# Probabilities with adjoining key columns for each transpose, and mask matmuls of 64 columns

## The chip, the cores and the metric

The kernel runs on one core of a Trainium2 chip. The time is the device time of one execution in microseconds (us), the median of several runs. The engines run beside each other: TensorE (PE; its weight loads are shown as PEld), VectorE (DVE), ScalarE (ACT), GpSimd (POOL) and SyncE (SP), whose queue issues the transfers.

## What is computed

Three layers follow each other: an attention whose scores get a bias from a running sum, a gated feed-forward layer that also mixes along the sequence, and a second layer that mixes along the sequence with a cosine and a sine part. The change is in the attention alone (B, H, S, D = 4, 8, 576, 64):

```python
scores = scale * np.matmul(q, k.transpose(0, 1, 3, 2))
causal = np.triu(np.ones((S, S), dtype=bool), k=1)
cum = np.cumsum(np.maximum(s, 0.0), axis=-1)
bias = -(cum[:, :, :, None] - cum[:, :, None, :])
scores = np.where(causal, -1e9, scores + np.minimum(bias, 0.0))
attn = np.exp(scores - np.max(scores, axis=-1, keepdims=True))
attn = attn / (np.sum(attn, axis=-1, keepdims=True) + 1e-09)
x = np.matmul(attn, v)
```

Then x goes through the feed-forward layer (x @ w_in, Gelu, a normed gate mixed by w_sg, @ w_out, plus x), and through theta = x @ w_theta, the sequence mixing of x cos(theta) and x sin(theta), and a last product with w_ch.

## The kernel before

Float32 products are made of float32r parts, a rounded high part and the rest: three matmuls for each product (high by low, low by high, high by high). All of them are recorded at one line (L106), so they are told apart by their tiles.

**Attention by pairs.** The 32 heads go in 16 pairs of two; the 64 dimensions of the first head lie in partitions 0 to 63, those of the second in 64 to 127, so the score matmuls of the two heads use different rows of TensorE and run side by side. The 576 queries are cut into five row tiles t (QS, QE: first row and causal end; t = 0 has 64 rows of its own, the others 128), and a row tile has only QE[t] keys: 64, 192, 320, 448 or 576.

**Scores (`score_units`).** Two groups of tiles fill the four PSUM banks of the tile `sc` in turn: (4, 1, 0), then (3, 2). For each tile there are three products and then the mask matmuls, bf16, which add a large negative number (mlow by mpick) to the keys behind each query: two masks for t = 1 to 4 (one for each block of 64 keys on the diagonal), one for t = 0, each for both heads. So far each mask covers 128 columns, of which 64 get zeros. VectorE then takes bias and scores together (L344: C plus scores, with the row minimum into negm) into E, and ScalarE takes the exponential in place, with the row sum (L350).

**The tile E.** It holds 1600 columns for each of the two heads, the heads interleaved: `E = [P, 1600, 2]`, so that one head's columns lie 8 bytes apart.

**Transposes (`transpose_units`).** E must be turned around for the product with v. TensorE does this with an identity: 128 columns of E are loaded as weights, and the identity is streamed through (L375, 25 for each pair, into PSUM tiles T of 512 columns; one more turns the reciprocals r). Blocks are named by row tile t and key block kt (kt = 0: the first 64 keys, where both heads share one transpose: the 64 keys of two heads interleaved are 128 adjoining columns; kt = 1 to 4: 128 keys of one head). ScalarE and VectorE copy T out to Ef and E0 (L383 to L404). `pv_units` then makes the product with v0 (first 64 keys, both heads in one block-diagonal tile) and vr.

**Order.** `attention` writes the steps of pair p's scores, pair p-1's transposes and pair p-2's product in a fixed order (ORDER, ORDER_V). Between the steps `pace` takes matmuls of the feed-forward layer of the batch before, as far as a credit of estimated nanoseconds allows; there is none of it for the first four pairs. Pieces of weight conversion are put in by a plan (PLAN). The build then lays out each engine's queue with a simulated timeline (`schedule_with_timeline_sim=True`); `row` keeps the score matmuls of a group together.

**After attention**, near 335 us, the last batch's feed-forward layer, the output products (wo), theta and the second layer follow (yo, th, co); none of their lines is touched.

## Time and profile before

| | |
|---|---|
| median of 3 runs | 674.57 us (673.63 to 678.18) |
| the profiled execution | 674.18 us |
| its span, first to last instruction | 672.3 us |
| mean granted TensorE clock | 0.986 |
| busy: PE, PEld, DVE, ACT, POOL | 634.8, 556.9, 427.4, 363.2, 179.0 us |
| transfers | 83.57 MB, 124 GB/s on the mean |

The span is that of the instructions; 1.9 us of the profiled execution lie around it. Busy times add up the stretches in which at least one instruction of the engine is under way; matmuls overlap, so a row of equal ones is read by the distance between them. The 40 slices of the page are 16.8 us each; attention takes the first twenty.

### The profile page before, as it was taken

Reading aid. Unit: us, or ns where it says so; the run is one execution under the profiler, and the core shown is the slowest. Engines: PE = TensorE matmul, PEld = TensorE weight load, DVE = VectorE, ACT = ScalarE, POOL = GpSimd, SP = SyncE. Lnnn points to the kernel's source line nnn. Section 1 sums busy time; section 2 is a strip of 40 time slices with the busy share of each in tenths; the row PEclk is TensorE's granted clock in tenths of the full one; section 3 lists DMA queues with packets and bytes.
Section 4 is the critical chain, followed back from the end, with each engine's and each line's share of the span. In section 5 each row is a group of like instructions: output and inputs, shape, how many; then the busy total and the mean of one; then the engine's idle time right before and its main releaser. Section 6 shows DMA issues by size and latency. Waiting matters only on the chain.

```text
span 672.3 us, 12581 instructions
## 1 busy us (share of the span) xinstructions
PE 634.8 (94%) x4676; PEld 556.9 (83%) x4676; DVE 427.4 (64%) x1048; ACT 363.2 (54%) x836; POOL 179.0 (27%) x203
## 2 busy tenths in 40 slices
PE   5889989989999999999997888999999999999997
PEld 4666667778777888778787788898999999989997
DVE  5578856765567563773259977887773477458412
ACT  3767768774688844775155435565550454245100
POOL 4234532433314423044397633220000100100000
PEclk9989999999999999999999889999999999999999
DMA  4556753266632565201355879831001200300101
GB/s 145 190 182 215 233 163 120 77 191 207 203 104 74 169 190 185 73 31 63 119 144 162 266 244 356 264 109 61 1 1 70 73 0 36 106 1 1 71 1 71
DMA packets 50189, 83.57 MB, mean 124 GB/s; under 512 B 8432, under 2 KB 20176, under 8 KB 50128
## 3 DMA queue, kind: packets, MB, share of 16 engines
q1 hardware_dynamic: 50128, 82.76, 38.4%
q8 instruction: 37, 0.61, 0.4%
q14 instruction: 24, 0.20, 0.1%
HBM read 61.61 MB, written 21.13 MB: 123 GB/s over the span
## 4 chain that ended last, share of the span: by engine, by line
PE 65%; ACT 10%; DMA 8%; DVE 8%; POOL 4%; issue 4%; SPq 1%; DVEq 0%; ACTq 0%; POOLq 0%
PE yo L106 17%; PE fo L106 13%; PE th L106 8%; PE co L106 8%; PE wo L106 6%; PE Y L106 4%; PE sc L106 4%; PE T L375 4%; ACT E L350 3%; POOL vT L653 2%; DMA wraw<-in_moe_w_tok_i 1%; PE tp L802 1%; DMA wraw<-in_moe_w_tok_r 1%; DMA wraw<-wd 1%; ACT vT L701 1%
## 5 line engine op out<-in xcount | busy, mean ns | idle before, releaser
L350 ACT ACTIVATE E<-E,negm 128x576 f32<-128x576 f32 (+4 forms) x160 | 92.8, 587 | 2.3 <-DVE negm L344 2.1
L106 PE MATMUL yo<-wkh,zh 128*128 128x288 f32 x288 | 85.3, 296 | 0.2 <-DVE x2T L875 0.2
L106 PE MATMUL yo<-wkl,zh 128*128 128x288 f32 x288 | 85.2, 296 | 0.0
L106 PE MATMUL yo<-wkh,zl 128*128 128x288 f32 x288 | 85.2, 297 | 0.0
L344 DVE CUSTOM_DVE_ANT_0 E<-sc,C 128x576 f32<-128x576 f32 (+4 forms) x160 | 68.2, 486 | 13.5 <-PE sc L106 11.3
L375 PE MATMUL T<-ident,E 128*128 128x128 f32 x400 | 64.2, 292 | 11.1 <-ACT Ef L383 5.6
L375 PEld LDWEIGHTS T<-ident,E 128*128 128x128 f32 x400 | 54.0, 193 | 17.1 <-ACT Ef L383 8.8
L106 PE MATMUL fo<-x,wih 128*128 128x288 f32 x256 | 56.0, 304 | 1.4 <-ACT uT L721 1.4
L106 PEld LDWEIGHTS yo<-wkh,zh 128*128 128x128 f32 x288 | 54.1, 188 | 0.7 <-DVE x2T L875 0.4
L106 PEld LDWEIGHTS yo<-wkl,zh 128*128 128x128 f32 x288 | 54.1, 188 | 0.3
L106 PEld LDWEIGHTS yo<-wkh,zl 128*128 128x128 f32 x288 | 54.0, 188 | 0.1
L106 PE MATMUL co<-u,wch 128*128 128x288 f32 x256 | 53.0, 295 | 0.0
L99 POOL TENSOR_SCALAR xt<-x2s 128x128 fp32r<-128x128 f32 x16 | 10.8, 688 | 155.8 <-DVE x2s L103 155.8
L106 PE MATMUL wo<-gh,woh 128*128 128x288 f32 x128 | 39.3, 310 | 8.1 <-ACT gh L95 4.7
L106 PEld LDWEIGHTS fo<-x,wih 128*128 128x128 f32 x256 | 41.8, 188 | 4.0 <-ACT uT L721 2.2
L106 PE MATMUL fo<-wih,x 128*128 128x512 f32 x128 | 43.3, 404 | 1.3 <-ACT x L95 0.7
L387 DVE COPY Ef<-T 128x512 f32<-128x512 f32 x32 | 21.8, 684 | 34.9 <-PE T L375 31.5
L106 PE MATMUL th<-wth,x2s 128*128 128x512 f32 x128 | 42.9, 400 | 0.0
L95 ACT CAST u<-x2T 128x576 fp32r<-128x576 f32 x16 | 10.7, 672 | 59.3 <-DVE x2T L875 59.3
L106 PE MATMUL sc<-kl,qh 64*128 64x288 f32 (+1 forms) x192 | 39.0, 397 | 3.0 <-DVE negm L344 3.0
L106 PEld LDWEIGHTS co<-u,wch 128*128 128x128 f32 x256 | 41.7, 188 | 0.0
L297 POOL TENSOR_TENSOR kl<-K,kh 128x576 fp32r<-128x576 f32 x15 | 21.8, 1452 | 67.2 <-ACT kh L95 36.9
(193 smaller groups left out, 1775.7 us busy)
## 6 DMA issues: line engine op xcount, KB each, us to landing
C<-cd SPq DMA_DIRECT2D x15, 576.0 KB, 6.1
Q<-in_q SPq DMA_DIRECT2D x16, 288.0 KB, 3.8
K<-in_k SPq DMA_DIRECT2D x16, 288.0 KB, 3.9
xT<-rd SPq DMA_DIRECT2D x32, 144.0 KB, 2.9
xd<-xT SPq DMA_DIRECT2D x16, 288.0 KB
gd<-uT SPq DMA_DIRECT2D x16, 288.0 KB, 4.4
gr<-gd SPq DMA_DIRECT2D x16, 288.0 KB
xr<-xd SPq DMA_DIRECT2D x16, 288.0 KB, 3.5
```

Of the source, the lines that this page charges most:

```text
L95: nc.scalar.copy(out, src)
L99: nc.gpsimd.tensor_scalar(out, src, 1.0, 1.0, op0=ALU.mult, op1=ALU.mult)
L106: return self.nc.tensor.matmul(out, lhsT, rhs, start=start, stop=stop)
L297: low = nc.gpsimd.tensor_tensor(kl, K, f32(kh), op=ALU.subtract)
L344: nc.vector.tensor_tensor_reduce(at.rearrange("p (i n) -> p i n", i=m), o[:, :, j], C[:, j, 0:n].rearrange("p (i n) -> p i n", i=m), -1.0, ...
L350: nc.scalar.activation(at, at, AF.Exp, bias=negm[:, j, c:c + 1], scale=-1.0, accum_out=sm[:, j * 5 + c:j * 5 + c + 1])
L375: nc.tensor.transpose(T[:, col:col + P], e, self.ident)
L387: nc.vector.tensor_copy(Ef[:, 512:1024], T)
L653: nc.gpsimd.tensor_scalar(vT[0:r, t], vT[0:r, t], rs[0:r, t:t + 1], nm[0:r, t:t + 1], op0=ALU.mult, op1=ALU.add)
L701: nc.scalar.activation(vT, vT, AF.Gelu_apprx_tanh)
L802: nc.tensor.transpose(tp[0:r, dt * P:(dt + 1) * P], x2T[:, dt, a:a + r], self.ident)
```

## The change

E becomes one row of 3200 columns. Of each row tile the first head's keys stand first, in blocks of 64 in falling order, then the second head's in rising order. So 128 keys of one head adjoin (the first head's two blocks swapped), and the two heads' first 64 keys meet in the middle and adjoin as well. VectorE writes the first head's blocks in falling order with a pattern of 64-column blocks. To match, the host swaps the two halves of each 128 rows of v for the even heads, and the transfers into v0 put the second head's 64 rows below the first's instead of between them. The PSUM tile `sc` gets the head as its outer index, row tile 4's two halves become adjoining columns across the border of two banks (its first half moves to column 224, row tile 1 to column 0), and each mask matmul has just the 64 columns of its own block; mpick shrinks from 192 columns to 64. Nothing is added and no order is written differently.

```diff
--- before.py
+++ after.py
@@ -28,9 +28,11 @@
 QS = [0, 64, 192, 320, 448]
 QR = [64, 128, 128, 128, 128]
 QE = [64, 192, 320, 448, 576]
-EOFF = [0, 64, 256, 576, 1024]
-
-GROUPS = [[[(4, 0, 288, 0), (1, 0, 192, 288)], [(4, 288, 288, 0), (0, 0, 64, 288)]],
+EOFF = [0, 128, 512, 1152, 2048]
+
+
+
+GROUPS = [[[(4, 0, 288, 224), (1, 0, 192, 0)], [(4, 288, 288, 0), (0, 0, 64, 288)]],
           [[(3, 0, 448, 0)], [(2, 0, 320, 0)]]]
 
 
@@ -147,7 +149,7 @@
 
 
         low = self.cum.tile([P, 2, P], F32, name="low")
-        pick = self.cum.tile([P, 3, 64], F32, name="pick")
+        pick = self.cum.tile([P, 64], F32, name="pick")
         nc.gpsimd.memset(low, 0.0)
         nc.gpsimd.memset(pick, 0.0)
         for i in (0, 64):
@@ -158,13 +160,13 @@
                     base=-64 * m, channel_multiplier=-1
                 )
             nc.gpsimd.affine_select(
-                out=pick[r, 1], in_=pick[r, 1], pattern=[[1, 64]], compare_op=ALU.not_equal, fill=NEG,
+                out=pick[r], in_=pick[r], pattern=[[1, 64]], compare_op=ALU.not_equal, fill=NEG,
                 base=0, channel_multiplier=-1
             )
         self.mlow = c.tile([P, 2, P], BF16, name="mlow")
         nc.vector.tensor_copy(self.mlow, low)
-        self.mpick = c.tile([P, 192], BF16, name="mpick")
-        nc.vector.tensor_copy(self.mpick, pick.rearrange("p m n -> p (m n)"))
+        self.mpick = c.tile([P, 64], BF16, name="mpick")
+        nc.vector.tensor_copy(self.mpick, pick)
         self.gcol = c.tile([P, 4], F32, name="gcol")
         self.halfpi = c.tile([P, 1], F32, name="halfpi")
         nc.vector.memset(self.halfpi, math.pi / 2)
@@ -282,7 +284,7 @@
         v0 = self.v0[pr % 3]
         for j in (0, 1):
             js = slice(c + j * D, c + j * D + D)
-            nc.sync.dma_start(v0.rearrange("(k i) c -> i k c", i=2)[j, :, j * D:j * D + D], self.v[b, 0:64, js])
+            nc.sync.dma_start(v0[j * D:j * D + D, j * D:j * D + D], self.v[b, 0:64, js])
         nc.sync.dma_start(vr, self.v[b, 64:576, c:c + P].rearrange("(t p) c -> p t c", p=P))
         self.vop[pr] = v0, vr
 
@@ -309,14 +311,14 @@
         C = self.cums.pop(pr)
         negm = self.negm[pr % 2]
         sm, r = self.st[pr % 2]
-        E = self.Es[pr] = self.a2.tile([P, 1600, 2], F32, name="E", tag="E")
+        E = self.Es[pr] = self.a2.tile([P, 3200], F32, name="E", tag="E")
         halves = [slice(j * D, j * D + D) for j in (0, 1)]
 
         for group in GROUPS:
             calls, sums, cost = [], [], 0.0
-            four = self.psS.tile([P, 2, 2, 512], F32, name="sc", tag="sc")
+            four = self.psS.tile([P, 2, 1024], F32, name="sc", tag="sc")
             for i, bank in enumerate(group):
-                o = four[:, i]
+                o = four[:, :, i * 512:i * 512 + 512]
                 for t, a, n, col in bank:
                     w = max(n, P)
                     qs = slice(QS[t], QS[t] + P)
@@ -329,24 +331,23 @@
                                           k == 0, k == 2 and not masks))
                     for m in masks:
                         for j, js in enumerate(halves):
-                            calls.append((o[:, j, col + w - P:col + w], self.mlow[js, m],
-                                          self.mpick[js, 64 - 64 * m:192 - 64 * m], False, m == masks[-1]))
+                            at = col + w - P + 64 * m
+                            calls.append((o[:, j, at:at + 64], self.mlow[js, m], self.mpick[js], False, m == masks[-1]))
                     if a == 0:
-                        sums.append((t, four[:, :, :, 0:n] if t == 4 else four[:, i:i + 1, :, col:col + n]))
+                        sums.append((t, four[:, :, i * 512 + col:i * 512 + col + QE[t]]))
                     cost += 3 * max(107.0, w / 2.4) + 120 * len(masks) + 120
             self.row(calls)
             for t, o in sums:
                 c = (t - 1) % 5
                 n = QE[t]
                 for j in (0, 1):
-                    at = E[:, EOFF[t]:EOFF[t] + n, j]
-                    m = o.shape[1]
+                    at = E[:, EOFF[t] + j * n:EOFF[t] + j * n + n].rearrange("p (b k) -> p b k", k=64)
                     nc.vector.tensor_tensor_reduce(
-                        at.rearrange("p (i n) -> p i n", i=m), o[:, :, j],
-                        C[:, j, 0:n].rearrange("p (i n) -> p i n", i=m), -1.0, BIG,
+                        at if j else at[:, ::-1], o[:, j].rearrange("p (b k) -> p b k", k=64),
+                        C[:, j, 0:n].rearrange("p (b k) -> p b k", k=64), -1.0, BIG,
                         ALU.add, ALU.min, negm[:, j, c:c + 1])
                 for j in (0, 1):
-                    at = E[:, EOFF[t]:EOFF[t] + n, j]
+                    at = E[:, EOFF[t] + j * n:EOFF[t] + j * n + n]
                     nc.scalar.activation(at, at, AF.Exp, bias=negm[:, j, c:c + 1], scale=-1.0,
                                          accum_out=sm[:, j * 5 + c:j * 5 + c + 1])
             if group is GROUPS[-1]:
@@ -370,9 +371,8 @@
 
         def transposed(T, j, blocks):
             for col, t, kt in blocks:
-                c = EOFF[t] + QS[kt]
-                e = E[:, c:c + P, j] if kt else E[:, c:c + 64].rearrange("p n j -> p (n j)")
-                nc.tensor.transpose(T[:, col:col + P], e, self.ident)
+                c = EOFF[t] + QE[t] - 64 if kt == 0 else EOFF[t] + (QE[t] + QS[kt] if j else QE[t] - QE[kt])
+                nc.tensor.transpose(T[:, col:col + P], E[:, c:c + P], self.ident)
 
         Efs = []
         for j in (0, 1):
@@ -1033,7 +1033,10 @@
     a = {n: np.asarray(inputs[n]) for n in _INS}
     a["q"] = a["q"].transpose(0, 1, 3, 2)
     a["k"] = a["k"].transpose(0, 1, 3, 2)
-    a["v"] = a["v"].transpose(0, 2, 1, 3).reshape(B, S, H * D)
+    v = a["v"].transpose(0, 2, 1, 3).copy()
+    even = v[:, 64:, ::2].reshape(B, 4, 2, 64, H // 2, D)
+    v[:, 64:, ::2] = even[:, :, ::-1].reshape(B, S - 64, H // 2, D)
+    a["v"] = v.reshape(B, S, H * D)
     a["s"] = a["s"].reshape(B * H, S).T
     for n in ("moe_w_sg", "moe2_w_tok_r", "moe2_w_tok_i"):
         a[n] = np.roll(a[n].T, (-64, -64), (0, 1))
```

## Rows read from the trace of the kernel before

**Rows 1.** The page: busy time, share of the span and instructions of each engine.

```profile
PE 634.8 (94%) x4676; PEld 556.9 (83%) x4676; DVE 427.4 (64%) x1048; ACT 363.2 (54%) x836; POOL 179.0 (27%) x203
```

**Rows 2.** Busy time by stretch, header first: attention's early part and the rest of it.

```profile
core 0: us, PE busy (x) PEld busy (x) DVE busy (x) ACT busy (x) POOL busy (x), PEclk, DMA share, GB/s
20.00:100.00 80.00, 69.90 (x570) 52.62 (x570) 59.15 (x172) 56.59 (x165) 30.92 (x27) 0.94 0.61 194
100.00:335.00 235.00, 229.25 (x1838) 188.52 (x1837) 140.20 (x424) 152.97 (x383) 75.56 (x84) 1.00 0.41 129
```

**Rows 3.** What PE waited for: total us, times, longest.

```profile
PE T L375 <- ACT Ef L383: 5.6, 4, 2.4
PE T L375 <- ACT E L350: 2.4, 2, 1.2
```

**Rows 4.** The page: shares of the chain that ended last, by line.

```profile
PE yo L106 17%; PE fo L106 13%; PE th L106 8%; PE co L106 8%; PE wo L106 6%; PE Y L106 4%; PE sc L106 4%; PE T L375 4%; ACT E L350 3%; POOL vT L653 2%; DMA wraw<-in_moe_w_tok_i 1%; PE tp L802 1%; DMA wraw<-in_moe_w_tok_r 1%; DMA wraw<-wd 1%
```

**Rows 5.** Tiles T and tp: durations in ns (min/median/max), first and last start, forms.

```profile
L375 PEld LDWEIGHTS T<-ident,E x400: 137/206/227, 19.7 to 329.6; 128*128 128x128 f32 x134
L375 PE MATMUL T<-ident,E x400: 270/283/490, 19.7 to 329.7; 128*128 128x128 f32 x134
...
L802 PEld LDWEIGHTS tp<-ident,x2T x80: 108/139/143, 416.8 to 603.4; 128*128 128x128 f32 x64, 128*64 128x64 f32 x16
L802 PE MATMUL tp<-ident,x2T x80: 270/272/327, 416.9 to 603.5; 128*128 128x128 f32 x64, 128*64 128x128 f32 x16
```

**Rows 6.** Timeline: start us, us, instructions merged; eight transposes of each kind.

```profile
307.97 1.11 PE L375 MATMUL T<-ident,E 128*128 128x128 f32 x8
...
416.93 1.04 PE L802 MATMUL tp<-ident,x2T 128*128 128x128 f32 x8
```

**Rows 7.** By form, then timeline: mask matmuls and the weight load behind them.

```profile
L106 PE MATMUL sc<-mpick,mlow 64*128 64x128 bf16 x288 | 24.4, 238 | 0.0
...
159.41 0.29 PE L106 MATMUL sc<-mpick,mlow 64*128 64x128 bf16 x4
...
160.46 0.23 PE L106 MATMUL sc<-mpick,mlow 64*128 64x128 bf16 x2
...
159.48 0.19 PEld L106 LDWEIGHTS sc<-kl,qh 64*128 64x128 f32 x2
```

**Rows 8.** ScalarE: the exponentials together, by form, and casts (busy us, mean ns).

```profile
L350 ACT ACTIVATE E<-E,negm 128x576 f32<-128x576 f32 (+4 forms) x160 | 92.8, 587 | 2.3 <-DVE negm L344 2.1
...
L350 ACT ACTIVATE E<-E,negm 128x576 f32<-128x576 f32 x32 | 26.6, 836 | 2.0 <-DVE negm L344 2.0
...
L350 ACT ACTIVATE E<-E,negm 128x64 f32<-128x64 f32 x32 | 10.9, 345 | 0.0
...
L95 ACT CAST u<-x2T 128x576 fp32r<-128x576 f32 x16 | 10.7, 672 | 59.3 <-DVE x2T L875 59.3
...
L95 ACT CAST wkh<-wta 128x288 fp32r<-128x288 f32 x18 | 7.7, 430 | 17.2 <-DVE wta L510 16.5 <-DVE mv L645 0.5
```

**Rows 9.** VectorE by form: score evacuation and a plain subtract.

```profile
L344 DVE CUSTOM_DVE_ANT_0 E<-sc,C 128x576 f32<-128x576 f32 x32 | 22.8, 750 | 4.0 <-DMA C<-cd 2.1 <-PE sc L106 1.8
...
L344 DVE CUSTOM_DVE_ANT_0 E<-sc,C 128x448 f32<-128x448 f32 x32 | 18.7, 620 | 9.5 <-PE sc L106 9.5
...
L344 DVE CUSTOM_DVE_ANT_0 E<-sc,C 128x64 f32<-128x64 f32 x32 | 5.8, 220 | 0.0
...
L103 DVE TENSOR_TENSOR u<-x2T,u 128x576 fp32r<-128x576 f32 x16 | 12.1, 755 | 5.9 <-ACT u L95 5.7
```

**Rows 10.** ScalarE: table loads of L350, and the Gelus by form.

```profile
L350 ACT ACT_TABLE_LOAD  x5: 1283/1283/1283, 114.2 to 284.2; - x5
...
L701 ACT ACTIVATE vT<-vT 128x2560 f32<-128x2560 f32 x3 | 7.0, 2338 | 0.0
...
L727 ACT ACTIVATE uT<-uT 128x2304 f32<-128x2304 f32 x3 | 6.4, 2127 | 0.0
```

**Rows 11.** Busy time by stretch around the lowest granted clock.

```profile
45.00:50.00 5.00, 2.48 (x19) 2.20 (x21) 5.00 (x12) 4.01 (x12) 4.37 (x5) 0.66 0.60 179
50.00:55.00 5.00, 5.00 (x36) 4.20 (x36) 4.72 (x18) 3.43 (x9) 1.29 (x1) 0.66 0.95 295
```

## Prediction

> **What bounds the kernel now.** I read five views in this order. First the busy times of the page: the matmul engine (PE) is busy 94% of the span, VectorE 64% and ScalarE 54% [rows 1]. Second the table by stretch, because the change lies only in the attention part, which ends near 335 us [rows 2]: from 100 to 335 us PE is busy 229.25 us, idle 5.75 of 235, so time taken out of its queue there comes off the end; from 20 to 100 us it is idle 10.1 of 80, so there its neighbours decide with it. Third PE's own waits: the longest, for ScalarE's copies of transposes (L383), is 5.6 us over the whole run, and the exponentials (L350) only 2.4 us [rows 3]. Fourth the chain that ended last, where the transposes (L375) take 4% of the span, the scores 4%, the exponentials 3% [rows 4]. Last the instructions themselves. A busy matmul row is not the same as its cost here: durations overlap, so I take cost from the pace of a run of equal instructions, not from their durations.
>
> **Transposes.** 400 of them a run, each a load of 128 columns of E and a matmul with the identity [rows 5]. Of the 25 of a pair, 20 read every second column (both heads lie interleaved) and 5 already read adjoining ones (the blocks with kt = 0, where both heads are wanted), so 320 change. The load takes 206 ns at the median for E, and 139 for the theta stage's transposes, whose 128 columns adjoin [rows 5]. Is that 67 ns on the path? No: a load runs under the matmul before it. Eight transposes of E in a row, all with step 2, last 1.11 us; eight with adjoining columns last 1.04 us [rows 6]. With the last matmul's own median taken off (283 and 272 ns), seven steps take 0.827 and 0.768 us: 118 against 110 ns, so 8.4 ns each. 320 x 8.4 = 2.7 us. A load that stands behind a drained engine, after a mask matmul for instance, can't hide; if one in each of 16 pairs pays the whole 67 ns, that is 1.1 us more. Ends: 0 and 3.8 us; 320 x 67 = 21 us would be right only if nothing overlapped, and the eight in a row exclude that. I take 2.7.
>
> [...]
>
> **Mask matmuls.** 288 of 128 columns become 288 of 64 [rows 7], always two heads side by side on different rows, so 144 steps. Each covers just its own block, no longer also a block of zeros. Four masks (two steps) last 0.29 us, two (one step) 0.23 us, so the second step adds 0.06 us [rows 7]; half as many columns can halve that to 0.03. Four of the five row tiles have two steps: 4 x 16 x 0.03 = 1.9 us. The last step of a tile is followed by a weight load of 0.19 us that begins before the mask ends (159.48 against 159.41 + 0.29) [rows 7], so its shortening is covered; without the cover it would be 80 x 0.03 = 2.4 us more. The trace has no bf16 mask of 64 columns, so the ends are 0 (the steps are paced by something other than their columns) and 4.3 us. I take 1.5, nearer to the half that is not covered.
>
> **Exponentials.** They read and write E at step 2 now and at step 1 afterwards. Their time grows from 345 ns for 64 columns to 836 for 576, 0.959 ns a column; the casts on the same engine, adjoining columns, from 430 for 288 to 672 for 576, 0.840 [rows 8]. If all the difference is the step, it is 0.119 x 51,200 columns (1600 a head, 32 heads) = 6.1 us of ScalarE; if it is the function or its accumulator, 0. On the path it counts far less: the matmul engine waited 2.4 us for exponentials in all [rows 3]. The chain has 3%, 20 us, of them [rows 4]; 6.1 of 92.8 us, 6.6%, of that is 1.3 us. I take 0.8, for the early pairs, where ScalarE is busy about 70% and PE has gaps [rows 2].
>
> **Score evacuation.** The VectorE instruction (L344) wrote at step 2 and will write adjoining columns, for the first head in runs of 64 in falling order. 220 ns for 64 columns and 750 for 576 are 1.035 ns a column, and a plain subtract of 576 adjoining columns takes 755 [rows 9]: step 2 already costs nothing, so nothing is gained. Can runs of 64 cost? The 576 form is two runs of 288 now, and lies at the 620 of 448 columns plus 128 x 1.035, 752, so a second run costs at most rounding, some 4 ns. A pair goes from 12 runs to 50, and 38 x 16 x 4 ns = 2.4 us of VectorE, which is idle 20.8 of the 80 us and 94.8 of the 235 [rows 2]: 0 on the path, and 0.5 if the early pairs, with a fifth of the work, have no room for it. That tile's two halves now adjoin across a PSUM bank border instead of lying in two banks; the instruction is still one, and both heads keep banks of their own.
>
> **Edits at nothing.** No instruction is added, and no DMA changes its count, its size or its place on SP's queue; of the transfers into v0 only the partitions change. mpick shrinks to a third before the first mask. The reordering of v is in the host's layout. No semaphore wait is added that could hold a queue: each exponential still waits for its own head's minimum, each transpose for its head's exponentials.
>
> **The sum.** 2.7 + 1.5 + 0.8 = 5.0 us off 674.18 us, the profiled execution (672.3 us of span and 1.9 around it), which lies 0.4 below the median of 674.57: 669.2. What is late next is the matmul engine itself, with its feed-forward work behind every saved step.
>
> **Rivals.**
> *All of it counts, 664 us.* The loads that can't hide, the second mask step and half of the exponentials' 6.1 us all reach the end: 3.8 + 3.2 + 3.0 = 10.0. For it: from 20 to 100 us the chain runs through ScalarE and transposes in turn [rows 4], and shorter exponentials free the score banks' users earlier. Against: 2.4 us of waiting for exponentials in 672.
>
> *The step is free or covered, 674 us.* The change does not do what it says: the load differs for another reason than the step (a wait on E, another engine writing E), or feed-forward work paces each stretch anyway. That is 0 to 1.5 us off, 673 to 674. [...] For it: feed-forward matmuls are packed between the groups, so a transpose's load often hides under one. Against: the first load behind such a matmul hides, the seven behind it did not [rows 6].
>
> *Order, slower, 684 us.* The build lays out each engine's order by a simulated timeline, and cheaper masks and a new overlap of E's parts can move a large ScalarE instruction ahead of exponentials. The large ones are the Gelus of the feed-forward half: a table load of 1.283, 2.338 us, and another table load of 1.283 before the exponentials go on, 4.9 us in all; vT's and uT's, three times each, make six places [rows 10]. PE waits little on them now; it decides from the third that falls between an exponential and a transpose for which PE has nothing else: 3 x 4.9 - 5.0 = 9.7 us slower than 674.2. For it: PE already waits 5.6 us for ScalarE copies of transposes [rows 3]. Against: feed-forward matmuls fill such holes, as the 5.75 us idle in 235 show [rows 2].
>
> A smaller risk lies in the range: the granted clock was 0.66 from 45 to 55 us, where PE was busy only 2.48 us of the first 5 [rows 11]. [...]
>
> **How the numbers follow.** A measurement of this kernel tells about 1% from no change, 6.7 us. Forecast, 2 to 6.7 us off: 0.50. All of it counts: 0.26. Free or covered: 0.15. Order: 0.09. Predicted 669.2; its own range is 667 to 673. For 8 in 10 the range takes in the upper rival's end (10 to 12 us off, 662) and a clock stretch or one displaced Gelu above no change (674 + 3.4, 677), leaving out the order rival and the extremes. Faster by over 1% is the second case, 0.26; within 1% the first and third, 0.65; slower by over 1% the last, 0.09.
>
> **What would show it.** Load of E down from 206 to about 140 ns, eight transposes in a row at 1.04 us; two mask steps near 0.26 us; the exponential of 576 columns below 800 ns if the step was its cost; the evacuation still 750 ns; attention's end near 329 us instead of 334, the rest unchanged. The prediction is wrong if the spacing of transposes stays at 118 ns, if the runs of 64 lengthen L344, or if idle time of PE from 100 to 335 us grows past 10 us.

## The result and the profile after

The changed kernel takes 665.57 us (median of 6 runs, 664.56 to 667.71) against 676.25 us (673.63 to 679.69, 6 runs) for the kernel before, measured beside it: a ratio of 0.9845, 95% interval 0.9823 to 0.9867, or 10.7 us. A second measurement of the same kernel (e8 below) gave 0.9865 [0.9839, 0.9890], 9.1 us (7.7 by the medians alone). The forecast was 669.2 with a range of 662 to 677: direction and range hold, but the time lies past the forecast's own range of 667 to 673, and the drop of 1.55% is of the class that was given 0.26, not of "within 1%", which was given 0.65. About half of it was never in the sum.

The profiled execution of after took 667.71 us, the longest of its six (span 666.0, clock 0.987); that of before, 674.18 us, lies near the lower end of its own six. So their spans lie 6.3 us apart, not 10.7, and what the traces are asked to explain is smaller than what was measured. Its page, the table by stretch and two of the matmul engine's waits answer to [rows 1 to 3]. First the page (busy time, share, instructions):

```profile
PE 629.3 (94%) x4676; PEld 552.0 (83%) x4676; DVE 427.1 (64%) x1048; ACT 359.8 (54%) x836; POOL 179.2 (27%) x203
```

The same kernel's table by stretch, with the columns of [rows 2]:

```profile
20.00:100.00 80.00, 69.69 (x568) 51.93 (x569) 56.99 (x171) 55.03 (x164) 31.17 (x27) 0.94 0.62 197
100.00:335.00 235.00, 230.03 (x1862) 188.63 (x1862) 141.01 (x425) 152.55 (x386) 80.13 (x89) 1.00 0.42 131
```

And what its matmul engine (PE) waited for:

```profile
PE T L375 <- ACT Ef L383: 3.6, 3, 1.6
...
PE T L375 <- ACT E L351: 1.9, 2, 1.1
```

PE is still 94% busy and idles 4.97 us in 100 to 335 us, where it idled 5.75 [rows 2]; the wait for ScalarE's copies went from 5.6 to 3.6 us, that for exponentials from 2.4 to 1.9 [rows 3]. So the shares hardly move. The changed instructions do. The load of tile T (ns, minimum/median/maximum), answering to [rows 5]:

```profile
L375 PEld LDWEIGHTS T<-ident,E x400: 137/140/230, 19.5 to 324.4; 128*128 128x128 f32 x134
```

Eight transposes in a row, then masks of one pair, from its timeline (start us, us, instructions merged), answering to [rows 6, 7]:

```profile
303.02 1.03 PE L375 MATMUL T<-ident,E 128*128 128x128 f32 x8
...
157.42 0.23 PE L108 MATMUL sc<-mpick,mlow 64*128 64x64 bf16 x4
...
157.86 0.20 PE L108 MATMUL sc<-mpick,mlow 64*128 64x64 bf16 x2
```

The exponentials together, then they, evacuation and masks by form (busy us, mean ns, idle before), answering to [rows 7 to 9]:

```profile
L351 ACT ACTIVATE E<-E,negm 128x576 f32<-128x576 f32 (+4 forms) x160 | 88.4, 555 | 1.5 <-DVE negm L345 1.2
...
L351 ACT ACTIVATE E<-E,negm 128x576 f32<-128x576 f32 x32 | 24.6, 772 | 1.4 <-DVE negm L345 1.2
L351 ACT ACTIVATE E<-E,negm 128x64 f32<-128x64 f32 x32 | 10.8, 338 | 0.0
...
L345 DVE CUSTOM_DVE_ANT_0 E<-sc,C 128x576 f32<-128x576 f32 x32 | 22.8, 751 | 2.1 <-PE sc L108 2.1
...
L108 PE MATMUL sc<-mpick,mlow 64*128 64x64 bf16 x288 | 20.3, 206 | 0.0
```

Each local sign that the prediction named is there: the load of E takes 140 ns instead of 206, eight transposes 1.03 us instead of 1.11, four masks 0.23 instead of 0.29 and two 0.20 instead of 0.23, the longest exponential 772 ns instead of 836, the evacuation 751 instead of 750. Attention's last product ends at 328.9 us instead of 334.1, just where the prediction had it. That is luck in these two traces: 2.8 of the 5.2 us open between pairs 7 and 9, in a way that it did not have, and none before pair 7.

**Where the time went.** The start of the 576-column evacuation that opens each head pair serves as a stopwatch for the whole attention part. VectorE's timeline shows it for pairs 7, 8, 9 and 15 (the first counted as 0). Before:

```profile
124.16 0.74 DVE L344 CUSTOM_DVE_ANT_0 E<-sc,C 128x576 f32<-128x576 f32 x1
...
145.75 0.75 DVE L344 CUSTOM_DVE_ANT_0 E<-sc,C 128x576 f32<-128x576 f32 x1
...
165.85 0.75 DVE L344 CUSTOM_DVE_ANT_0 E<-sc,C 128x576 f32<-128x576 f32 x1
...
295.55 0.74 DVE L344 CUSTOM_DVE_ANT_0 E<-sc,C 128x576 f32<-128x576 f32 x1
```

After:

```profile
124.21 0.74 DVE L345 CUSTOM_DVE_ANT_0 E<-sc,C 128x576 f32<-128x576 f32 x1
...
143.40 0.75 DVE L345 CUSTOM_DVE_ANT_0 E<-sc,C 128x576 f32<-128x576 f32 x1
...
163.11 0.75 DVE L345 CUSTOM_DVE_ANT_0 E<-sc,C 128x576 f32<-128x576 f32 x1
...
290.85 0.74 DVE L345 CUSTOM_DVE_ANT_0 E<-sc,C 128x576 f32<-128x576 f32 x1
```

From pair 7 to pair 8 before takes 21.59 us and after 19.20: 2.4 us in one pair. From pair 9 to pair 15 it is 129.70 against 127.73 (differences here are taken from unrounded starts), 0.33 us a pair, and every one of the six gains. Up to pair 7 the two executions do not differ (124.16 and 124.21). Two kinds of gain, then: one spread over the later pairs, as the prediction had it, and one in a single place that it did not have.

That place is the matmul engine's, from 135 to 150 us: busy 13.20 us of 15 in before, 14.78 in after. In before PE stands still at 142.1 us until the transposes go on, which wait for ScalarE:

```profile
143.79 0.62 PE L375 MATMUL T<-ident,E 128*128 128x128 f32 x3 [1.66 <-ACT Ef L383]
```

Follow that wait back. ScalarE's timeline of before, up to the copy that is waited for:

```profile
137.82 0.39 ACT L721 COPY uT<-fo 128x288 f32<-128x288 f32 x1
138.58 0.67 ACT L95 CAST x<-xT 128x576 fp32r<-128x576 f32 x1 [0.36 <-DVE xT L432]
139.27 1.28 ACT L727 ACT_TABLE_LOAD   x1
140.56 2.13 ACT L727 ACTIVATE uT<-uT 128x2304 f32<-128x2304 f32 x1
142.82 0.43 ACT L95 CAST wsrh<-gt 128x288 fp32r<-128x288 f32 x1
143.16 0.58 ACT L383 COPY Ef<-T 128x512 f32<-128x512 f32 x1
```

The same work in after:

```profile
136.76 0.39 ACT L721 COPY uT<-fo 128x288 f32<-128x288 f32 x1
137.10 0.43 ACT L97 CAST wsrh<-gt 128x288 fp32r<-128x288 f32 x1
137.55 1.28 ACT L727 ACT_TABLE_LOAD   x1
138.85 2.14 ACT L727 ACTIVATE uT<-uT 128x2304 f32<-128x2304 f32 x1
140.89 0.56 ACT L383 COPY Ef<-T 128x512 f32<-128x512 f32 x1
```

The copy stands behind uT's Gelu in both; in after the Gelu begins 1.71 us earlier, no rounding of x stands right ahead of it, and the rounding of wsrh, the last half of the feed-forward gate's mixing weights, has gone before it. That rounding needs its data. SP's timeline of before, four rows of the stretch 135 to 139 us (gt<-in_moe_w_sg at L596 is that last load, in two parts):

```profile
135.19 0.38 SPq L267 DMA_DIRECT2D Q<-in_q  x1
136.53 0.49 SPq L596 DMA_DIRECT2D gt<-in_moe_w_sg  x1
137.10 1.19 SPq L411 DMA_DIRECT2D xT<-rd  x2
138.34 0.59 SPq L596 DMA_DIRECT2D gt<-in_moe_w_sg  x1
```

and of after:

```profile
133.75 1.12 SPq L596 DMA_DIRECT2D gt<-in_moe_w_sg  x2
134.92 0.58 SPq L269 DMA_DIRECT2D Q<-in_q  x1
...
137.60 1.10 SPq L411 DMA_DIRECT2D xT<-rd  x2
```

There the load has gone ahead of Q and of the two xT transfers; in before only its first part was ahead of xT. In this trace of before the load itself holds little: the rounding begins 0.13 us after the Gelu's end (142.69 to 142.82). The Gelu's place, and the rounding between it and the copy, hold the rest. No line of the diff touches the Gelu, the rounding or the load. The build lays out every engine's queue by a simulated timeline, and the shorter matmuls move it. They move much else with it: the two kernels' orders on PE differ in some 260 places, most of them between 40 and 80 us.

Theory: 5 us come from layout and masks, as predicted, and the rest from the new order; that the place is this one, and what holds PE there, was read from the first traces and then tried. Rivals: the layout is worth more than was counted (exponentials, loads that don't hide), or the narrow masks are.

### The profile page after: what moved, and what is told of

The parts are those of the page before. It is cut to its first block, busy times and chain, and to the rows that moved or that the text cites. A ratio compares the mean times of both kernels' runs of the same rounds, so it can differ in the third digit from the quotient of the medians.

```text
span 666.0 us, 12580 instructions
## 1 busy us (share of the span) xinstructions
PE 629.3 (94%) x4676; PEld 552.0 (83%) x4676; DVE 427.1 (64%) x1048; ACT 359.8 (54%) x836; POOL 179.2 (27%) x203
## 4 chain that ended last, share of the span: by engine, by line
PE 70%; ACT 7%; DVE 7%; DMA 6%; POOL 4%; issue 4%; SPq 1%; POOLq 0%; DVEq 0%; ACTq 0%
PE yo L108 17%; PE fo L108 15%; PE th L108 8%; PE co L108 8%; PE wo L108 7%; PE sc L108 5%; PE Y L108 5%; PE T L375 4%; ACT E L351 3%; POOL vT L653 2%; PE tp L802 1%; DMA wraw<-wd 1%; DMA K<-in_k 1%; DMA xT<-rd 1%; DMA v<-in_v 1%
## 5 line engine op out<-in xcount | busy, mean ns | idle before, releaser
L351 ACT ACTIVATE E<-E,negm 128x576 f32<-128x576 f32 (+4 forms) x160 | 88.4, 555 | 1.5 <-DVE negm L345 1.2
L375 PE MATMUL T<-ident,E 128*128 128x128 f32 x400 | 61.9, 289 | 8.7 <-ACT Ef L383 3.6
L375 PEld LDWEIGHTS T<-ident,E 128*128 128x128 f32 x400 | 48.5, 147 | 13.9 <-ACT Ef L383 5.2
L387 DVE COPY Ef<-T 128x512 f32<-128x512 f32 x32 | 21.9, 685 | 36.8 <-PE T L375 32.1
```

The costliest lines, as they stand in the source:

```text
L351: nc.scalar.activation(at, at, AF.Exp, bias=negm[:, j, c:c + 1], scale=-1.0, accum_out=sm[:, j * 5 + c:j * 5 + c + 1])
L375: nc.tensor.transpose(T[:, col:col + P], E[:, c:c + P], self.ident)
L387: nc.vector.tensor_copy(Ef[:, 512:1024], T)
```

## The experiments

Ratios are against the kernel before, run on the same chip beside them: 676.87 us in the first four, 676.43 in the next four, 676.08 in the three after these, 677.33 beside the last. "Off" is what the ratio makes of that median; the ratio on record can differ from the quotient of the two medians by up to 0.24%.

**The two halves of the change.** e1 keeps the old layout and takes only the narrow masks:

```
-  calls.append((o[:, j, col + w - P:col + w], self.mlow[js, m],
-                self.mpick[js, 64 - 64 * m:192 - 64 * m], False, m == masks[-1]))
+  at = col + w - P + 64 * m
+  calls.append((o[:, j, at:at + 64], self.mlow[js, m],
+                self.mpick[js, 64:128], False, m == masks[-1]))
```

> The old interleaved E with mask matmuls of 64 columns alone. The engines' queues then stand in the same order as in the changed kernel, which the masks' width alone sets. Theory of terms (transposes 2.7, masks 1.5 to 1.9, exponentials 0.8 us, the rest of the 10 us noise): about 674 us against 676 before, and two mask steps near 0.26 us. Theory of order (the queues' new order, not the steps' cost, brings about half of the gain): about 670 us, with the early pairs and the stretch behind attention ahead of before. Theory of exponentials (step 1 instead of step 2 frees ScalarE and that reaches the end): 674 us, since E keeps its step.

e2 takes the new layout with masks of 128 columns, the same edit the other way round.

> The new layout of E with the old mask matmuls of 128 columns; the queues stand in the order of the kernel before. Theory of terms: 676 less 2.7 for transposes and 0.8 for exponentials, about 672.5 us; loads of E at 140 ns and eight transposes in a row at 1.04 us. Theory of order: about 671 to 672 us, the other half of the gain missing. Theory of exponentials: 667 us, nearly all of the gain without the masks.

e1: 670.83 us, 0.9907 [0.9879, 0.9934], 6.3 us off. e2: 673.22 us, 0.9945 [0.9919, 0.9970], 3.7 us off. Together 10.0, which is all of the change. The masks alone bring more than the layout, although each is just 0.03 us a step shorter. The order of the instructions tells why: on ScalarE and SP e1 has exactly the order of after (on PE but for two neighbouring records near 62 us, which differ between two runs of after as well), and e2 exactly that of before. Between these four kernels the width of a mask matmul alone decides which order the build lays out. In e2 the load came later than the Gelu's end: ScalarE waited 2.91 us for it, with the copy behind, and PE stood for 4.24 us. From ScalarE's and PE's timelines of e2:

```profile
145.44 0.43 ACT L97 CAST wsrh<-gt 128x288 fp32r<-128x288 f32 x1 [2.91 <-DMA gt<-in_moe_w_sg]
```

```profile
146.41 0.90 PE L376 MATMUL T<-ident,E 128*128 128x128 f32 x3 [4.24 <-ACT Ef L384]
```

Three transposes take 0.90 us where before's took 0.62, at a granted clock of 0.50 in that stretch. PE by stretches of 2 us in e2 (busy time, count, granted clock, DMA share, GB/s):

```profile
144.00:146.00 2.00, 0.00 (x0) 0.94 0.32 90
146.00:148.00 2.00, 1.59 (x7) 0.50 0.40 120
148.00:150.00 2.00, 2.00 (x14) 0.71 0.00 0
```

After the idle stretch the granted clock was 0.50 for 2 us and 0.71 in the next 2, before it stood at 1.00 again: an estimated 1.6 us lost at the rate of the full clock. So in e2 the late load cost a wait, and a fall of the clock followed. In before's own trace it cost 0.13 us on ScalarE, and the clock stayed at 1.00.

**The step of the transposes by itself.** e3 is the kernel before with its interleaved E, whose transposes of the blocks with kt above 0 read 128 adjoining columns of it, so that a block holds both heads' columns; e4 is the changed kernel whose same transposes read every second column of 256 instead.

```
-  e = E[:, c:c + P, j] if kt else E[:, c:c + 64].rearrange("p n j -> p (n j)")
+  c += 64 * j if kt else 0
+  e = E[:, c:c + 64].rearrange("p n j -> p (n j)")
```

```
-  nc.tensor.transpose(T[:, col:col + P], E[:, c:c + P], self.ident)
+  if kt:
+      c = min(c, EOFF[t] + 2 * QE[t] - 256)
+      e = E[:, c:c + 256].rearrange("p (n i) -> p n i", i=2)[:, :, 0]
+  else:
+      e = E[:, c:c + P]
+  nc.tensor.transpose(T[:, col:col + P], e, self.ident)
```

> The kernel before, in which each transpose with kt of 1 to 4 reads 128 adjoining columns of the interleaved E, that is 64 keys of both heads, so the product with v mixes keys: the output is not the reference's, but each instruction has its shape and E, VectorE's writes and the exponentials keep step 2. It waits for both heads' exponentials, so some of the queues' order differs. Theory of terms: 676 less 2.7, about 673.5 us, with the load at 140 ns. Theory of exponentials: also 673.5, and the new layout with old masks lies 5 us or more below it. Theory of order: within 2 us of before.

> The changed kernel, in which each transpose with kt of 1 to 4 reads every second column of 256 (keys of one or both heads of the same row tile), so the product with v takes wrong keys: the output is not the reference's. VectorE's writes, the exponentials and the masks stay as changed. Theory of terms: 2.7 to 3.8 us above the changed kernel, about 668.5 to 669.5 us, load at 206 ns. Theory of exponentials: the same 2.7, with the exponential of 576 columns still as fast as in the changed kernel. Theory of order: the order differs somewhat from the changed kernel's, so 666 to 673 us.

e3: 673.25 us, 0.9935 [0.9914, 0.9957], 4.4 us off. e4: 668.08 us, 0.9874 [0.9844, 0.9903], which is 0.6 to 2.0 us short of after's two measurements (0.9845, 0.9865), within the intervals, and less than the 2.7 to 3.8 expected. The load's row of e3:

```profile
L376 PEld LDWEIGHTS T<-ident,E x400: 137/140/230, 19.8 to 328.5; 128*128 128x128 f32 x134
```

In e4 the same row's median is 207. Of the load only the reading differs, and its time follows it both ways: 206 to 140, 140 to 207 ns. The distance from one transpose of a row to the next, over some 160 of them from 150 to 335 us, is 109 ns in e2, e3 and after, and 116 on the mean (118 at the median) in before, e1 and e4, where the fifth that adjoined already is among them. The times of e3 and e4 are less clean: the new reads also moved the queues' order, on PE between 20 and 90 us alone, so the times can't be put down to the reading. In e3 the exponentials still take 835 ns at 576 columns, in e2 770; their ratios, 4.4 and 3.7 us off, can't tell what that is worth. The table below tells more, since its last column lies where these orders are alike.

**Whose wait is it?** e5 is the kernel before with the rounding of wsrh's second half on GpSimd, so that ScalarE's copies no longer stand behind it; e6 is the same in the changed kernel.

```
-  self.rnd("act", self.wsrh[:, c], g)
+  self.rnd("pool" if k == 9 else "act", self.wsrh[:, c], g)
```

> The kernel before with one instruction on another engine: the last rounding of the mixing weights for the gate (wsrh, second half), which waits for its transfer near 138 to 145 us, goes to GpSimd, so ScalarE's queue no longer stands behind that transfer; every other queue keeps its order. Theory of the held queue: the copy of transposed columns behind it starts 2 to 5 us earlier and the time falls by 2 to 4.5 us, to 672.5 to 675 us against some 676.5. Theory that the masks' own cost brings the 6 us of the first experiment: no change, within 1 us.

> The same move of one rounding to GpSimd in the changed kernel, where its transfer is issued some 4 us earlier and has landed when ScalarE comes to it. Theory of the held queue: nothing to gain, within 1 us of the changed kernel. If moving it helps here as much as in the kernel before (2 us or more), the held queue is not what sets the two kernels apart.

e5: 677.61 us, 1.0008 [0.9990, 1.0027]; e6: 666.65 us, 0.9839 [0.9818, 0.9860], as after. So the theory that the rounding in ScalarE's queue holds PE falls. With the rounding gone from there, PE still idles in e5, twice:

```profile
143.36 0.61 PE L375 MATMUL T<-ident,E 128*128 128x128 f32 x3 [1.09 <-ACT Ef L383]
145.37 0.66 PE L375 MATMUL T<-ident,E 128*128 128x128 f32 x4 [1.13 <-DVE Ef L387]
```

The first wait is the Gelu's: the copy starts at 142.74, as it ends. The second is the load's: VectorE's copy (L387) stands behind its subtract for wsrl, which needs the rounding, and GpSimd's rounding waits for the transfer:

```profile
143.80 0.43 POOL L99 TENSOR_SCALAR wsrh<-gt 128x288 fp32r<-128x288 f32 x1 [2.51 <-DMA gt<-in_moe_w_sg]
```

So there are two holders, the Gelu and the load, and the later one decides. The next runs move them one by one.

**The load put late in the changed kernel.** e7 puts both parts of the last load behind the xT transfers, where before has the second; e8 is the changed kernel again, beside it. In the cut, last_r is the second of the xT transfers.

```
+  with ExitStack() as es:
+      if k == 9:
+          es.enter_context(self.tc.issue_after(self.last_r.ins))
       nc.sync.dma_start(g[i:i + 64], self.w_sg[512:576, c])
```

> The changed kernel with the two small loads of that rounding's weights put behind the two loads of reciprocals (xT) on SP's queue, as in the kernel before; ScalarE's rounding then stands behind the first copy of transposed columns instead of ahead of the Gelu, and otherwise the order is that of the changed kernel. Theory of the held queue: the rounding holds the next copies for 0 to 3 us, so 0 to 3 us slower than the changed kernel, less than the whole 4 us since the first copy is ahead of it. Theory of masks: no change.

> The changed kernel again, beside the three others on the same chip: about 665.5 us, and the kernel before about 676.5.

e7: 670.92 us, 0.9895 [0.9875, 0.9916]. e8: 668.72 us, 0.9865 [0.9839, 0.9890]; e6, on the same chip, 0.9839. So the late place, later than before's, costs 2.0 to 3.8 us of the gain; the interval of e7 lies apart from e6's and overlaps e8's. The Gelu is early here (136.89 us) and can't be it. In the trace PE waits for the rounding by name, and the clock falls afterwards. PE's timeline of e7, then its stretches of 2 us:

```profile
142.29 0.40 PE L108 MATMUL fo<-wsrh,vh 128*128 128x288 f32 x1 [1.50 <-ACT wsrh L97]
```

```profile
144.00:146.00 2.00, 2.00 (x11) 0.50 0.02 4
146.00:148.00 2.00, 2.00 (x12) 0.65 0.00 0
```

**Load and Gelu put early in the kernel before.** This is the other direction, with nothing of the change in it. e9 lets the load's second part pass the xT transfers, so that both parts are ahead of them; every other queue keeps before's order.

```
+  with ExitStack() as es:
+      if k == 9:
+          es.enter_context(self.tc.high_priority())
       nc.sync.dma_start(g[i:i + 64], self.w_sg[512:576, c])
```

> The kernel before, unchanged but for one place on SP's queue: the second of the two last mixing-weight loads goes ahead of the two xT transfers instead of behind them, about 1.2 us earlier; every other engine's order is that of before. If the late load is what makes the matmul engine idle near 140 us, the second load lands 1.2 us earlier, the engine idles about 1 us less in 135 to 150 us, and the time is 1 to 2 us below before's (ratio 0.997 to 0.999). If the queue's order only goes along with the gain, the ratio is 1.000.

e10 draws the plan of the mixing weights forward by one place in pair 7 (G loads, H rounds):

```
-  7: ("H5 G7", "H6 G8", "H7 G9", "H8 H9"),
+  7: ("H5 G7 H6 G8", "H7 G9", "", "H8 H9"),
```

> The kernel before with the plan of the mixing weights drawn forward by one place in head pair 7 (G8 and H7 earlier, so that their buffer comes free earlier and both last loads go ahead of the xT transfers); old layout of E and masks of 128 columns. Theory of the late load: the rounding of the last half of the mixing weights comes 2 to 5 us earlier, the matmul engine is busy 14 us or more of 135 to 150 us, and the kernel is 3 to 5 us below before (ratio 0.993 to 0.9955), with nothing of the layout changed. Rival, that the gain over the counted terms comes with the new layout and the narrow masks elsewhere in the queues: ratio 0.998 to 1.001.

e11 is the same plan in the changed kernel.

> The changed kernel with the same plan, drawn forward by one place. Theory of the late load: the load is early there already, so nothing is left to gain: ratio as after's, 0.984 to 0.988. Rival, that the earlier plan gives something of its own: 0.980 or less.

e9: 674.61 us, 0.9979 [0.9965, 0.9994], 1.4 us off for one swap on one queue. e10: 673.07 us, 0.9957 [0.9941, 0.9974], 2.9 us off, just under the 3 to 5 expected. e11: 667.36 us, 0.9879 [0.9858, 0.9900]: the changed kernel gains nothing from the same plan, and e11 against e10 is 5.3 us, worked out from the two ratios: the change with the load early on both sides, though e10 keeps some of the wait. In e10's trace SP issues both parts at 136.06, ahead of xT at 137.28, and the Gelu begins 15.42 us after pair 7's start (16.01 in e9, 16.41 in before), but half of PE's wait of 1.66 us is left. It is the Gelu's, which ends just ahead of the rounding at 141.56 and the copy:

```profile
142.51 0.61 PE L375 MATMUL T<-ident,E 128*128 128x128 f32 x3 [0.84 <-ACT Ef L383]
```

e12 therefore takes both off ScalarE in e10: the rounding goes to GpSimd, as in e5, and the one copy to VectorE. PE's order moves with it in some places between 140 and 160 us.

```
+  if pr == 6 and j:
+      nc.vector.tensor_copy(Ef[:, 0:512], T)
+  else:
       nc.scalar.copy(Ef[:, 0:512], T)
```

> The kernel of e10 (old layout, masks of 128 columns, plan of the mixing weights forward by one place), in which the two things that stand behind uT's Gelu on ScalarE near 142 us leave ScalarE: the rounding of the last half of the mixing weights goes to GpSimd, and the one copy of transposes that the matmul engine waits 0.84 us for goes to VectorE. Account of two holders (the load, and the Gelu with its table load in front of that copy; the later one decides): the rest of the wait goes too, pair 7 to pair 8 falls from e10's 20.4 us to 19.5 to 19.9, what the narrow masks alone have, and the kernel is 3.3 to 4.5 us below before (0.9935 to 0.995). Account of the load alone: the wait that is left in e10 belongs to the load, so it only changes its name to the rounding on GpSimd, pair 7 to 8 stays at 20.2 us or more and the ratio is e10's, 0.9957 with its interval.

e12: 671.84 us, 0.9934 [0.9914, 0.9953], 4.5 us off, and the profile has no wait of PE left from 139 to 150 us. The account of two holders forecast 3.3 to 4.5; the load alone, e10's 2.9. The ratio is at the first's end, though the intervals of e12 and e10 overlap; the table decides it. Of the twelve none beats the changed kernel: e6's 0.9839 lies inside its interval.

**The table that sorts them.** From the starts of the pairs' first evacuations in each profiled execution: pair 7 to pair 8, where the copies and the load are waited for; pair 8 to 9; and pair 9 to 15, where only steady work lies. PE is its busy time from 135 to 150 us.

| kernel | load on SP | PE | pair 7 to 8 | 8 to 9 | 9 to 15 |
|---|---|---|---|---|---|
| before | second part late | 13.20 | 21.59 | 20.10 | 129.70 |
| e5, rounding moved | second part late | 12.77 | 22.08 | 21.24 | 129.81 |
| e9, both parts ahead of xT | less late | 13.59 | 20.95 | 20.10 | 129.74 |
| e10, the same and the Gelu earlier | less late | 14.02 | 20.37 | 20.10 | 129.71 |
| e12, e10 with both off ScalarE | less late | 14.97 | 19.39 | 19.90 | 129.77 |
| e3, adjoining reads alone | second part late | 12.15 | 22.22 | 21.01 | 128.94 |
| e2, whole layout | second part late | 10.76 | 24.55 | 19.75 | 128.42 |
| e7, after with the load late | both parts late | 13.27 | 21.45 | 21.04 | 127.70 |
| e1, masks | early | 14.56 | 19.71 | 20.01 | 128.88 |
| e4, after with step 2 | early | 14.51 | 19.76 | 19.92 | 128.47 |
| after | early | 14.78 | 19.20 | 19.71 | 127.73 |
| e8, after again | early | 14.82 | 19.15 | 19.67 | 127.69 |
| e6, after, rounding moved | early | 14.89 | 18.90 | 19.70 | 127.68 |
| e11, after, plan forward | early | 14.75 | 19.24 | 19.68 | 127.66 |

The last column follows the change's parts and not the load: the five kernels with nothing of it lie within 0.11 us, the five with all of it within 0.07. In six pairs the adjoining reads are worth 0.76 (before to e3) and 0.74 (e4 to after), the masks 0.82 (before to e1) and 0.69 (e2 to after), the rest of the layout 0.52 (e3 to e2) and 0.41 (e1 to e4); since the evacuation keeps its time, that is put down to the exponentials. At the same rate in all sixteen pairs that is 2.0, 2.0 and 1.2 us: 5.2, an estimate from six pairs. Against e12, which has neither wait, the four measurements of the changed kernel (0.9839 to 0.9879, the moved rounding and plan counted in) are 3.7 to 6.4 us lower, which takes it in.

For the early pairs the rate is not shown. From pair 0 to 7 the five kernels with nothing of the change take 107.9 to 111.3 us and the five with all of it 107.3 to 109.8, with falls of the granted clock at different places (0.50 in before from 34 to 36 and from 48 to 52 us, in after from 48 to 52 and from 92 to 94). There the new order also costs something: pair 3 to 4 takes 15.0 us in each of the five with before's order, 14.7 to 16.3 in the five with after's, and 16.3 in e1, which has just the masks.

Pair 7 to 8 follows the two holders and not the change: e12, which has nothing of the change, takes 19.39 us, 2.2 less than before, and e7, which has all of it, 21.45. The steps between them show the holders apart, with the Gelu's begin counted from pair 7's start. From before to e9, 0.64 us, the rounding's 0.13 us of idle time goes and the Gelu begins 0.4 earlier. From e9 to e10, 0.58 us, the load is waited for in neither and the Gelu begins 0.59 earlier. The rest, 0.98 us, goes with e12. Pair 8 to 9 holds a second price: 21.0 to 21.2 in e3, e5 and e7, where the clock fell after the wait (to 0.57 and 0.58 in two stretches of 2 us in e3, to 0.50 and 0.65 in e5 and e7), 19.7 to 20.1 elsewhere (in e2 the fall lies ahead of pair 8's start). So the late load costs 2.3 us in e7 against e8 from pair 7 to 8, and 1.4 more from pair 8 to 9, behind the fall of the clock.

## Why the prediction was right, and where it failed

**What bounds the kernel: right.** Time taken out of PE's queue came off the end, at 0.33 us a pair in the pairs from 9 to 15.

**Transposes, 2.7 us: right, somewhat high.** By pace they give 320 x 7 to 9 ns = 2.2 to 2.9 us, by the pairs an estimated 2.0. The 21 us of a load that hides nowhere is excluded, as the eight in a row [rows 6] had excluded it. The load that can't hide, which the prediction put at up to 1.1 us and then left out of its 2.7, is there: from 150 to 335 us a step in a row of transposes takes 220 to 226 ns ten times in before, and 164 to 166 eight times in after, mostly the first step behind a mask. So some 56 of the 66 ns show there, about 0.6 us for the ten; the pairs' 2.0 has it in already.

In e3 and e4 only the step of the load's read changes, and the load goes from 206 to 140 ns in e3 and from 140 to 207 in e4. So the rival that the step is free falls.

**Masks, 1.5 us: right for what they cost, wrong for what they do.** Four masks went from 0.29 to 0.23 us and two from 0.23 to 0.20 [rows 7], so the second step fell from 0.06 to 0.03 us, as halved columns had it; the first fell by 0.03 as well, and how much of that the weight load behind it covers, no row shows. By the pairs that is an estimated 2.0 us. But e1 took 6.3 us off.

**Exponentials, 0.8 us: right, somewhat low.** ScalarE's busy time on them fell by 4.4 us (92.8 to 88.4), and an estimated 1.2 of it reach the end by the pairs, unevenly: from e1 to e4 the gain lies in two of the six, 0.17 and 0.23 us. In these two PE waits, not for exponentials by name but for VectorE's xT and ScalarE's copies of uT. The whole step was put at 6.1 us; from 338 ns for 64 columns to 772 for 576 are 0.848 ns a column, where it was 0.959, so nearly all of that slope's difference from the casts' 0.840 [rows 8] was the step.

**Evacuation at nothing: right.** 751 ns for 576 columns, in runs of 64 and in falling order for one head, against 750 at step 2 [rows 9]; VectorE's busy time is 427.1 against 427.4 us.

**The step that failed** stands under "Edits at nothing": "no DMA changes its count, its size or its place on SP's queue", and with it all that the sum leaves out. Count and size stayed, the place did not, nor did ScalarE's order: the shorter mask matmuls alone moved the last mixing-weight load from behind Q, and in its second part behind xT, to ahead of them, and uT's Gelu to an earlier start. Undoing the late places in before, without the change, is worth 4.5 us by e12's ratio, 2.9 by e10's. The traces show less of it: from pair 7 to 9 e12 is 2.4 us shorter than before. Before's profiled execution is 3 us faster than the median of those beside e12, and the clock stayed at 1.00 there after the wait, where in e2, e3, e5 and e7 it fell to between 0.50 and 0.57; whether before's other executions paid that is not shown. By these numbers the sum should have been 5.2 and 2.4 to 4.5, that is 7.6 to 9.7; the two measurements are 10.7 and 9.1.

The rival "Order, slower" had this mechanism, its source (the simulated timeline), its instruction (a Gelu of uT, one of the six places) and the row in which it shows, PE's 5.6 us of waiting for ScalarE's copies [rows 3]. It had the wrong sign. It asked only whether a Gelu could move ahead of something; that row, followed back, leads to a Gelu that already stood ahead of a copy, so the order could also get better, and 2.0 of the 5.6 us went. "All of it counts", 664, came out nearest in time and is wrong in its cause: of its 10 us the changed instructions brought some 5.2. Its term of 3.2 us for the masks is also worked out nowhere in the prediction.

No run shows as a loss of time the 3.4 us of a clock stretch, which the range's upper end of 677 uses; shown are granted clocks: 0.66 over the 10 us of [rows 11], an estimated 3.4 us against the rate of the full clock, and 0.50 and 0.71 in two stretches of 2 us of e2, an estimated 1.6.

**What stays open.** In the profiled executions 1.1 us more of the gap opens between 334 and 410 us, past attention; e10's trace has 0.9 us of it against before as well, e9's goes the other way, and the runs do not tell an effect from the scatter. The two profiled executions lie 6.3 us apart where 9.1 to 10.7 were measured, and no trace shows the rest. The price of the Gelu's place was not tried in a run of its own; the steps from e9 to e10 and to e12 are the nearest. Why the simulated timeline orders these queues as it does was not taken apart; shown is only that the masks' width decides it.

## What to carry to other kernels

Where a build lays out the queues from its own estimates of durations, a shorter instruction changes orders that no line of the diff touches: before pricing an edit at nothing, follow each of the bound engine's longest waits back to the queue places behind it, and price its removal as well as its growth. Undo an edit in halves, and compare the halves' queue orders before their times: here the half with the smaller cost carried the larger gain. Where stages repeat, the spacing of their starts in one trace tells tenths of a microsecond where medians tell two or three: here a gain spread evenly over like stages, 0.33 us a pair, was the instructions' own; one that opened in a single stage, 2.4 us, was a wait, and moving that wait's source alone, in both directions, settled it.

## What the runs showed of the hardware

- A weight load of 128 float32 columns of E took 140 ns at the median from adjoining columns (after, e3) and 206 to 207 from every second one (before, e4); a row of loads with their matmuls went at 109 ns a step (e2, e3, after) against 116 to 118 (before, e1, e4), so nearly all of the 66 ns was hidden. In some steps, mostly the first of a row behind a mask, 56 of them showed: 164 to 166 ns in after against 220 to 226 in before.
- The exponential of 576 columns, float32 read and written, took 836 ns on ScalarE at step 2 (835 in e3) and 772 from adjoining columns (770 in e2 and e4): 64 ns, or 0.11 ns a column. VectorE's evacuation of 576 columns took 750 ns where it wrote at step 2 and 751 where it wrote adjoining columns.
- In four traces two stretches of 2 us at a lower granted clock stood behind a wait of PE: 0.50 and 0.71 in e2 after 4.24 us, 0.57 and 0.58 in e3 after 2.9, 0.50 and 0.65 in e7 and in e5, whose longest single waits near there were 1.50 and 1.13 us. In before's profiled execution the clock stood at 1.00 after a wait of 1.66 us. The wait's length alone does not tell these cases apart.
- The last mixing-weight load, two transfers of 64 x 288 float32, landed at very different distances from its issue. From the issue of its later part to the rounding, for which ScalarE stood idle, it was 6.8 us in e2 (138.63 to 145.44, the DMA share 0.84 to 1.05 in the stretches of 2 us from 136 to 144); from the issue of its first part 5.2 us in e7 (136.66 to 141.81), and at most 3.4 in after (133.75 to 137.10, with no wait for it).
